# Attention scores mirrored once per sequence, and z turned later: one core of Trainium2

## The chip, the cores and the metric

The kernel runs on one core of a Trainium2 chip. The metric is the device time of one execution in microseconds (us). A core has five engines that run side by side and wait for each other through semaphores: TensorE (PE in the profile, with its weight loads as a lane of their own, PEld), VectorE (DVE), ScalarE (ACT), GpSimd (POOL) and SyncE (SP). SyncE and GpSimd also issue the DMA transfers, each from a queue of its own that works in order.

## The reference

There are 8 sequences of 2816 tokens. Attention without a softmax comes first, and its output is routed through a mixture of experts:

```python
scores = scale * np.matmul(z, z.transpose(0, 2, 1))   # z: 8 x 2816 x 64
attn = np.maximum(scores, 0.0) ** 2
x = u * np.matmul(attn, v)                            # u, v: 8 x 2816 x 256
...
y_dense = np.maximum(x @ w1_dense, 0.0) @ w2_dense
expert_idx = np.argmax(x @ w_gate, axis=1)            # 8 experts
y_moe = gate_w * (np.maximum(x @ w1[e], 0.0) @ w2[e]) # for the rows of expert e
out = y_dense + y_moe
```

What matters for this case: the scores are z times its own transpose, so the matrix of a sequence is symmetric. The block of scores of tokens i against tokens j is the transpose of the block of j against i.

## The kernel before

A sequence is 22 blocks of 128 tokens (`nK`). Six *groups* per sequence (`groups`) take 2, 4, 4, 4, 4 and 4 of these blocks as queries; a group's tile `A` holds relu-squared scores of all 22 key blocks against the group's queries. Three buffers hold `A` in turn, so group n + 3 overwrites group n.

`scores` makes one tile of scores: it takes a pair of PSUM banks, and TensorE multiplies blocks of `zT` (L390), keys as weights, the group's queries as the moving operand. 64 rows of the array carry the even key blocks and 64 the odd ones, side by side. `relu` then has ScalarE or VectorE take the relu into `r` (L405, L407), and ScalarE, VectorE or GpSimd the square into `A` (L418, L420). A tile of a four-block group is two matmuls of 512 columns; that of a two-block group is four of 256.

`av` makes the output of two query blocks: 88 matmuls of 256 columns with blocks of `A` as weights and `v` as the moving operand (L579), in two passes over the 22 key blocks. In between, `fill` puts in score tiles of this group or of the next two; `swap_rows` does so at the change of passes. At its end a VectorE multiplication by `u` (`gate_x`, L606, "the gate") writes `pays` and frees the output's banks, and SyncE turns the result into `xT` for the routing (L608). Ahead of each `av`, `load_u` has SyncE load `u` for two blocks further on into `ut` (L146), a tile with three buffers, so that a load waits for the gate of the `av` just ended.

Symmetry is used in part already: group n doesn't compute its scores against the keys of group n - 2 of its sequence (`far`). `far_steps` has SyncE transpose them by DMA (L468) out of `A` of group n - 2, into the place in `A` of group n where they belong. Before group n + 3 may be opened, these reads of group n's buffer have to be issued (`open_group`) and thought done (`read_at`).

The next sequence's z is loaded by GpSimd (`load_z`), copied by VectorE in two halves with each block doubled (`turn_z`, L113), and each half transposed by SyncE into `zT` (L116). Once the second half is issued, the sequence is entered in `z_there`, and from then on `ahead` may give out its scores.

All of this stands in an order that the kernel writes out itself at build time, for TensorE, ScalarE, VectorE and SyncE. A planner in the program keeps a clock of TensorE's work (`now`) and of the other engines (`free`), offers operations to them with guessed durations (`offer`, `best`, `run`), and so decides what is emitted next; each engine then runs its instructions in the emitted order. `tick(g)` runs what is due at block g: once in the middle of an `av` and once at its end. `soon(t, fn)` offers `fn` to VectorE at tick t. Here that holds the loads of z, v and the experts' weights (`wall`, 8 experts of 2048 columns) and the turns of z: the z load at block 0 of the sequence before, its turns at blocks 5 and 6, the loads of v from block 13, the weights from sequence 1 on at blocks 15, 18 and 21.

After the attention, the MoE stage (`slot`, `up`, `down`, `half`) runs over the tokens sorted by expert.

Of the kernel before, what the change touches and what calls it, by code (L numbers as in the profile page):

```python
# [15 lines left out]
P = 128  # L16
# [3 lines left out]
def kernel(  # L20
# [39 lines left out]
    WD = 2 * F + 4 * D  # L60
# [28 lines left out]
    wall = const.tile([P, E, WD], BF, name="wall")  # L89
# [13 lines left out]
    def load_z(b):  # L103
        z_of[b] = zpool.tile([P, nK, dq], BF, name="zr", bufs=1)
        nc.vector.memset(z_of[b][:, 0, 0:1], 0.0)
        nc.gpsimd.dma_start(out=z_of[b][:], in_=z[b].rearrange("(p k) d -> p k d", p=P))

    def turn_z(b, k0, k1):

        if k0 == 0:  # L110
            zn_of[b] = zpool.tile([P, nK, 2, dq], BF, name="zn", bufs=1)
            zT_of[b] = zpool.tile([P, nK, P], BF, name="zT")
        nc.vector.tensor_copy(  # L113
            zn_of[b][:, k0:k1, :, :],
            z_of[b][:, k0:k1, :].unsqueeze(2).to_broadcast([P, k1 - k0, 2, dq]))
        nc.sync.dma_start_transpose(  # L116
            out=zT_of[b][:, k0:k1, :],
            in_=zn_of[b][:, k0:k1].rearrange("p k h d -> p (k h d)"))
        if k1 == nK:
            z_there.add(b)  # L120

# [11 lines left out]
    now = [0.0]  # L133
# [4 lines left out]

    z_of, zn_of, zT_of, v_of, ut_of, xT_of, lg_of, rs = {}, {}, {}, {}, {}, {}, {}, {}

    def load_u(g, gate=False):
        ut = aw.tile([P, 2, D], F32, name="ut", bufs=3)
        if gate:
            nc.vector.memset(ut[:, 0, 0:1], 0.0)
        b, i = divmod(g, nK)
        nc.sync.dma_start(out=ut[:], in_=uf[:, b, i:i + 2, :])  # L146
        ut_of[g] = ut[:]


# [114 lines left out]
    A = {}  # L264
    groups = []
# [63 lines left out]
    def until(cond):  # L329

        while cond() is None:
            pick = best()
            assert pick is not None
            now[0] = max(now[0], pick[0][0])
            give(pick)
        now[0] = max(now[0], cond())
        run(now[0])
# [15 lines left out]
    def open_group(n):  # L353
        if n not in A:
            while turning and turning[0][0] <= n - 3:
                turning.pop(0)[1]()
            A[n] = aA.tile([P, nK, 4 * P], BF, name="A", tag="A")[:]
            w = groups[n][2]
            if w < 4:
                A[n] = A[n].rearrange("p k c -> p (k c)")[:, :nK * w * P]  # L360
                A[n] = A[n].rearrange("p (k c) -> p k c", k=nK)
# [78 lines left out]
        ts = [key_at.get((m, k)) for k in range(i0, i0 + w)]  # L440
        return None if None in ts else max(ts)

    def turned_to(a, n):

        _, j0, wj = groups[a]
        w = groups[n][2]
        flat = A[n].rearrange("p k c -> p (k c)")
        return flat[:, j0 * w * P:(j0 + wj) * w * P]

    def block(n, k, c):  # L450

        _, i0, w = groups[n]
        for a in far[n]:
            _, j0, wj = groups[a]
            if j0 <= k < j0 + wj:
                x = c * wj + k - j0
                return turned_to(a, n)[:, x * P:(x + 1) * P]
        return A[n][:, k, c * P:(c + 1) * P]

    def far_steps(a):  # L460

        _, j0, wj = groups[a]

        def step(n):
            _, i0, w = groups[n]
            assert a + 1 in A
            open_group(n)
            nc.sync.dma_start_transpose(  # L468
                out=turned_to(a, n).rearrange("p (x c) -> p x c", c=P),
                in_=A[a][:, i0:i0 + w, :].rearrange("p k c -> p (k c)"))  # L470
# [8 lines left out]
    turn_at = [0.0]  # L479
    read_at = {}  # L480
    jobs = []

    def fill(n, force=False):

        if jobs and jobs[0][0] <= now[0] and room(1):
            jobs.pop(0)[1]()
            return True
        m = ahead(n)
        busy = sum(1 for op in todo if op[0] in (1, 4))
        if m is not None and room(1) and busy <= (4 if n < 2 else 2):  # L490
            scores(m, left[m].pop(0))
            return True
        return False
# [59 lines left out]
    def av(n, i, between):  # L553
        b, i0, w = groups[n]
        if i == i0:
            turning.extend(far_steps(n))
        keep[0] = 0
        if n == 0 and i == i0:

            fill(n)  # L560
            need(n, 0)
        until(lambda: pairs[0][0] if pairs else None)
        ox = take_pair()
        o = banks(ox, "o")
        for p in range(2):
            rest = list(range(nK))
            for x in range(nK):
                k = rest[0]
                if i == i0 and p == 0:

                    k = min(rest, key=lambda k: (max(key_at.get((n, k), 9e9), v_at(n, k)), k))
                    need(n, k)
                rest.remove(k)
                if n == 0 and i == i0 and p == 0 and x in (12, 14, 16):
                    load_u(2 * (x - 12) // 2, gate=True)
                for h in range(2):
                    r = slice(h * dq, (h + 1) * dq)
                    j = p ^ h
                    nc.tensor.matmul(out=o[:, j, 0:D], lhsT=block(n, k, i + j - i0)[r],  # L579
                                     rhs=v_of[b][r, k, :], start=(p == 0 and x == 0),  # L580
                                     stop=(p == 1 and x == nK - 1))
# [12 lines left out]
        def done(t):  # L594
            give_pair(t + 0.1, ox)

        g = b * nK + i
        offer(now[0] + 0.2, 0, {"dve": (0.63, lambda eng: gate_x(g, o))}, done)
        keep[0] = 0


    def gate_x(g, o):
        g0 = g % (2 * G)
        x = pays[:, g0:g0 + 2, 0:D]
        assert g + 1 < 2 * G or (g - 2 * G in placed and g + 1 - 2 * G in placed)
        nc.vector.tensor_mul(x, o[:, :, 0:D], ut_of.pop(g))  # L606
        xT = aw.tile([P, 5, P], BF, name="xT", bufs=8)
        nc.sync.dma_start_transpose(  # L608
            out=xT[:], in_=pays[:, g0:g0 + 2, :].rearrange("p n r -> p (n r)")[:, 0:5 * P])
        for j in range(2):  # L610
            xT_of[g + j] = xT[:, 3 * j:3 * j + 2, :]

# [399 lines left out]
    def soon(t, fn, dur=0.07):  # L1012
        at(t, lambda: offer(now[0], 3, {"dve": (dur, lambda eng: fn())}))
# [19 lines left out]
    for e in range(E):  # L1033
# [62 lines left out]
    for q in range(nQ - 2):  # L1096
        t = starts[q + 1] - 1 + LAG
# [40 lines left out]
    for s in range(NT - MAYBE + 2):  # L1138
# [4 lines left out]
        if s % 3 == 1 and waiting:  # L1143
# [5 lines left out]
    n = nc.values_load(used[0:1, 0:1], min_val=0, max_val=NH,  # L1149
                       skip_runtime_bounds_check_because="made by the table")  # L1150
# [34 lines left out]
```

## Time and profile before

| | us |
|---|---|
| median of 3 runs | 883.23 (883.2 to 883.38) |
| the profiled execution | 883.35 |
| its span, first to last instruction | 881.2 |
| first to last matmul | 1.1 to 871.3 |
| end of the last attention output | about 555 |
| mean granted TensorE clock | 0.997 of full |

The profile's page gives busy time per engine, the chain of work that ended last, and groups of instructions by line with count, total and mean duration and the idle time ahead of them. Further views list stretches of time (busy time by engine, granted clock, the share of time in which the 16 DMA engines were busy), instructions in order of time, and waits. In a timeline "SPq" is SyncE's queue: the duration there is that of issuing a DMA, not of its transfer. Rows of instructions that follow each other are merged, "x32" being their number.

| SyncE's DMAs in the attention | line | count |
|---|---|---|
| `u` loads, 256 KB | L146 | 88 |
| `xT` transposes, 5 blocks of 128x128 | L608 | 88 |
| `A` to `A` transposes, 8 or 16 blocks | L468 | 32 |
| `zT` transposes, 11 blocks | L116 | 14 |

### The profile page before, as it was taken

The page shows a single profiled execution, that of the slowest core. Times are in us where ns is not written, and L with a number is a line of the kernel's source. Part 1 is how long each engine was busy: PE and PEld are TensorE (multiplying, and loading weights), DVE is VectorE, ACT ScalarE, POOL GpSimd, SP SyncE. Part 2 cuts the span into 40 slices and gives each one's busy share as a digit, 9 for nine tenths or more (in the row PEclk, how much of TensorE's full clock was granted, in tenths as well). Part 3 has the DMA queues.
Part 4 walks back from the last instruction along what each step waited for, and adds up shares of the span by engine and source line. Part 5 has one row for each costly group of instructions (what it writes and reads, how often), then busy time and mean ns, then how long its engine had stood idle before and what let it go on. Part 6 is the DMA issues. An engine that isn't in the chain of part 4 may idle for free.

```text
span 881.2 us, 30493 instructions
## 1 busy us (share of the span) xinstructions
PE 861.5 (98%) x12257; PEld 757.7 (86%) x12257; DVE 700.9 (80%) x1348; ACT 737.2 (84%) x913; POOL 491.6 (56%) x560
## 2 busy tenths in 40 slices
PE   7999999999999999999999999999999999999995
PEld 5788898898888888888888888888888888889994
DVE  7999999998999999999999996756665445446663
ACT  7999998998998998998998994577777777777773
POOL 8203355445426436436336334588888888877664
PEclk9999999999999999999999999999999999999998
DMA  8897988979979979989999976465646565533442
GB/s 155 148 151 139 161 162 149 185 165 173 181 161 185 167 165 185 162 181 143 198 182 165 165 135 115 104 136 131 136 122 120 121 123 122 124 103 103 95 98 76
DMA packets 258830, 127.62 MB, mean 145 GB/s; under 512 B 222846, under 2 KB 237438, under 8 KB 258688
## 3 DMA queue, kind: packets, MB, share of 16 engines
q1 hardware_dynamic: 227040, 70.23, 46.2%
q0 software_dynamic: 31648, 55.45, 29.6%
q8 instruction: 96, 1.57, 0.8%
q14 instruction: 46, 0.38, 0.1%
HBM read 61.54 MB, written 37.16 MB: 112 GB/s over the span
## 4 chain that ended last, share of the span: by engine, by line
PE 81%; POOL 6%; issue 4%; DVE 4%; DMA 2%; ACT 1%; SPq 0%; POOLq 0%; DVEq 0%; ACTq 0%
PE o L579 44%; PE h_ps L936 13%; PE yy L944 12%; PE s L390 10%; POOL out_dram L962 5%; DMA out_dram<-ring,ix 1%; DVE r L407 1%; PE lg L634 1%; POOL A L420 1%; DVE A L420 1%; ACT r L405 1%; DMA ring<-xs 1%; DVE pays L606 0%; ACT A L418 0%; DMA z<-in_z_dram 0%
## 5 line engine op out<-in xcount | busy, mean ns | idle before, releaser
L579 PE MATMUL o<-vb,A 64*128 64x256 bf16 x7744 | 491.1, 269 | 3.3 <-POOL A L420 1.7
L579 PEld LDWEIGHTS <-A 64*128 64x128 bf16 x7744 | 406.5, 94 | 53.7 <-POOL A L420 3.0
L724 POOL DMA_INDIRECT xs<-pays,pi x176 | 190.2, 1081 | 249.3 <-DVE pi L722 204.5
L405 ACT ACTIVATE r<-s 128x1024 f32<-128x1024 f32 (+1 forms) x268 | 263.8, 1012 | 21.6 <-PE s L390 19.2
L418 ACT ACTIVATE A<-r 128x1024 bf16<-128x1024 f32 (+1 forms) x263 | 266.6, 1046 | 7.1 <-DVE r L407 4.2
L939 ACT ACTIVATE ring<-h_ps 128x1024 bf16<-128x1024 f32 x180 | 184.1, 1024 | 89.6 <-PE h_ps L936 88.1
L407 DVE TENSOR_SCALAR r<-s 128x1024 f32<-128x1024 f32 (+1 forms) x164 | 197.6, 1215 | 6.5 <-PE s L390 1.9
L420 DVE TENSOR_TENSOR A<-r 128x1024 bf16<-128x1024 f32 x161 | 196.4, 1231 | 2.1 <-ACT r L405 1.7
L960 DVE SCALAR_TENSOR_TENSOR ring<-yy,me,ring 128x256 f32<-128x256 f32 x180 | 86.9, 483 | 124.6 <-ACT ring L959 84.7
L962 POOL DMA_INDIRECT out_dram<-ring,me x140 | 147.5, 1054 | 42.0 <-issue 24.4
L390 PE MATMUL s<-zT 64*128 64x512 bf16 (+1 forms) x944 | 156.8, 357 | 1.8 <-ACT zT L192 0.6
L944 PEld LDWEIGHTS <-ring 128*128 128x128 bf16 x1440 | 140.1, 98 | 16.1 <-issue 0.3
L944 PE MATMUL yy<-w2d,ring 128*128 128x256 bf16 x720 | 108.0, 273 | 0.1
L944 PE MATMUL yy<-ring 128*128 128x256 bf16 x720 | 108.0, 273 | 0.0
L936 PE MATMUL h_ps<-ring,w1d 128*128 128x256 bf16 x720 | 93.3, 272 | 1.0 <-DVE pays L606 0.8
L936 PE MATMUL h_ps<-ring 128*128 128x256 bf16 (+1 forms) x880 | 93.7, 253 | 0.0
L924 DVE COPY ring<-wall 128x2048 bf16 x110 | 79.7, 740 | 8.0 <-DVE ring L960 4.0
L936 PEld LDWEIGHTS <-ring 128*128 128x128 bf16 x880 | 74.3, 98 | 6.8
L936 PEld LDWEIGHTS <-w1d 128*128 128x128 bf16 x720 | 70.1, 98 | 9.3 <-issue 1.0
L390 PEld LDWEIGHTS <-zT 64*128 64x128 bf16 x944 | 57.6, 94 | 16.5 <-issue 2.6
L606 DVE TENSOR_TENSOR pays<-o,ut 128x512 bf16<-128x512 f32 x88 | 60.4, 687 | 14.0 <-PE o L579 13.7
L959 ACT COPY ring<-yy 128x256 f32<-128x256 f32 x180 | 65.9, 366 | 1.8 <-PE yy L944 1.8
(120 smaller groups left out, 370.0 us busy)
## 6 DMA issues: line engine op xcount, KB each, us to landing
ut<-in_u_dram SPq DMA_DIRECT2D x88, 256.0 KB
vb<-in_v_dram POOLq DMA_DIRECT2D x42, 192.0 KB
wall<-in_moe_w_dram POOLq DMA_DIRECT2D x16, 256.0 KB
xs<-pays,pi POOLq DMA_INDIRECT x176
zr<-in_z_dram POOLq DMA_DIRECT2D x7, 352.0 KB
out_dram<-ring,me POOLq DMA_INDIRECT x140
ring<-xs SPq DMA_TRANSPOSE x114
vb<-in_v_dram POOLq DMA_DIRECT2D x14, 128.0 KB
```

The lines of the kernel that those rows point to most:

```text
L390: nc.tensor.matmul(out=s[:, h, y * c:(y + 1) * c], lhsT=zT[r, k + h, :], rhs=zT[r, i0:i0 + w, :], start=True, stop=True)
L405: nc.scalar.activation(r[:, :, :c], s[:, :, :c], AF.Relu, scale=1.0 / S)
L407: nc.vector.tensor_scalar(out=r[:, :, :c], in0=s[:, :, :c], scalar1=1.0 / S, scalar2=0.0, op0=ALU.mult, op1=ALU.max)
L418: nc.scalar.activation(a, r, AF.Square)
L420: (nc.gpsimd if eng == "pool" else nc.vector).tensor_mul(a, r, r)
L579: nc.tensor.matmul(out=o[:, j, 0:D], lhsT=block(n, k, i + j - i0)[r], rhs=v_of[b][r, k, :], start=(p == 0 and x == 0), stop=(p == 1 and x ...
L724: ins = nc.gpsimd.indirect_dma_start(out=xs, out_offset=bass.IndirectOffsetOnAxis(ap=pi[:], axis=0), in_=pays[:, g % (2 * G), 0:ROW].bitca ...
L936: nc.tensor.matmul(out=h_ps[:, f, hs, :], lhsT=w1(c, f), rhs=xT[:, hs, c, :], start=(c == 0), stop=(c == 1))
L939: nc.scalar.activation(h, h_ps[:].rearrange("p f h t -> p f (h t)"), AF.Relu)
L944: nc.tensor.matmul(out=y[:, k, :], lhsT=h[:, f, j * P:(j + 1) * P], rhs=w2(f), start=(f == 0), stop=(f == 3))
L960: nc.vector.scalar_tensor_tensor(out=ys, in0=y[:, 1, :], scalar=me[:, j, 0:1], in1=yd, op0=ALU.mult, op1=ALU.add)
L962: ins = nc.gpsimd.indirect_dma_start(out=out, out_offset=bass.IndirectOffsetOnAxis(ap=ids[j], axis=0), in_=ys, in_offset=None, bounds_chec ...
```

## The change

Group 0 of each sequence but the last is now transposed into all later groups of its sequence from 2 on, not only into group 2. As the buffers of groups 3, 4 and 5 aren't there yet, these *mirrors* go into columns of `wall` that belong to the last two experts and are loaded later (`spare`, `mirror`); the mirrors for groups 4 and 5 are one transpose of 16 blocks, that for group 3 one of 8. `block` then gives the output matmuls their weights from there, and `left` holds three score tiles fewer per sequence. In sequence 7 no mirrors are made.

A new clock `sync` counts SyncE's guessed work: each DMA it issues adds a duration (`issue`). It takes the place of `turn_at` in deciding when the next transpose out of `A` may be issued; the time when a group's buffer is thought read (`read_at`) and when transposed scores are thought there (`key_at`) follow it too.

From sequence 1 on, z of the next sequence is loaded at block 7 in place of 0, and its halves are turned at blocks 10 and 13 in place of 5 and 6; sequence 0 keeps the old places. The weight loads of the last three halves of experts move into sequence 7, to blocks 4, 9 and 14, since the mirrors of sequence 6 must have been read by then.

```diff
@@ turn_z
         nc.sync.dma_start_transpose(
             out=zT_of[b][:, k0:k1, :],
             in_=zn_of[b][:, k0:k1].rearrange("p k h d -> p (k h d)"))
+        issue(1.5)
         if k1 == nK:
             z_there.add(b)
...
+    sync = [0.0]
+
+    def issue(dur, ready=0.0):
+        sync[0] = max(sync[0], now[0], ready) + dur
+
...
+    spare = wall[:].rearrange("p e w -> p (e w)")
+    mirror = {(0, 4): (E - 1) * WD, (0, 5): (E - 1) * WD + 8 * P, (0, 3): (E - 2) * WD + 2 * F}
+
+    def slots(b):
+
+        return list(mirror) if b < B - 1 else []
+
     left, far, key_at = {}, {}, {}
     for n, (b, i0, w) in enumerate(groups):
-        far[n] = [m for m in (n - 2,) if m >= 0
-                  if groups[m][0] == b]
+        far[n] = [m for m in range(max(n - 5, 0), n - 1)
+                  if groups[m][0] == b and (m == n - 2 or (m % 6, n % 6) in slots(b))]
...
-    def turned_to(a, n):
+    def turned_to(a, n, w):
 
         _, j0, wj = groups[a]
+        if a == n - 2:
+            flat = A[n].rearrange("p k c -> p (k c)")
+            return flat[:, j0 * w * P:(j0 + wj) * w * P]
+        x = mirror[a % 6, n % 6]
+        return spare[:, x:x + w * wj * P]
...
-        def step(n):
-            _, i0, w = groups[n]
-            assert a + 1 in A
-            open_group(n)
+        def step(ns):
+            n = ns[0]
+            i0, w = groups[n][1], sum(groups[m][2] for m in ns)
+            if n == a + 2:
+                open_group(a + 1)
+                open_group(n)
             nc.sync.dma_start_transpose(
-                out=turned_to(a, n).rearrange("p (x c) -> p x c", c=P),
+                out=turned_to(a, n, w).rearrange("p (x c) -> p x c", c=P),
                 in_=A[a][:, i0:i0 + w, :].rearrange("p k c -> p (k c)"))
-            turn_at[0] = now[0] + 0.17 * w * wj
-            read_at[a] = now[0] + 1.5 + 0.19 * w * wj
-            for j in range(wj):
-                key_at[n, j0 + j] = now[0] + 7.0
-
-        return [(a, lambda n=n: step(n), n) for n in (a + 2,) if a in far.get(n, [])]
+            issue(0.18 * w * wj, read_at.get(a - 1, 0.0) if n == a + 2 else 0.0)
+            read_at[a] = sync[0] + 3.5
+            for m in ns:
+                for j in range(wj):
+                    key_at[m, j0 + j] = sync[0] + 3.0
+
+        ns = [[n] for n in range(a + 2, min(a + 6, len(groups))) if a in far[n]]
+        if len(ns) == 4:
+            ns[2:] = [ns[2] + ns[3]]
+        elif groups[a][2] == 4:
+            ns = ns[1:] + ns[:1]
+        return [(a, lambda m=m: step(m), m[-1]) for m in ns]
...
-                if x in (3, 10, 17)[1 - p:] and turning and turn_at[0] <= now[0]:
+                if x in (3, 10, 17)[1 - p:] and turning and sync[0] <= now[0] + 0.5:
                     t = can_turn(turning[0][2], turning[0][0])
-                    if t is not None and t <= now[0] and turning[0][0] + 1 in A:
+                    if t is not None and t <= now[0]:
                         turning.pop(0)[1]()
...
-            soon(t, lambda b=b: load_z(b + 1))
-            soon(t + 5, lambda b=b: turn_z(b + 1, 0, nK // 2), 0.4)
-            soon(t + 6, lambda b=b: turn_z(b + 1, nK // 2, nK), 0.4)
+            soon(t + 7 if b else 0, lambda b=b: load_z(b + 1))
+            soon(t + 10 if b else 5, lambda b=b: turn_z(b + 1, 0, nK // 2), 0.4)
+            soon(t + 13 if b else 6, lambda b=b: turn_z(b + 1, nK // 2, nK), 0.4)
...
-    ts = [b * nK + x for b in range(1, B) for x in (15, 18, 21)][2:]
+    ts = [b * nK + x for b in range(1, B - 1) for x in (15, 18, 21)][2:-1]
+    ts += [(B - 1) * nK + x for x in (4, 9, 14)]
```

The `u` load and the `xT` transpose call `issue` too (0.6 and 1.25 us).

More of the change, by code (lines that the diff above doesn't have):

```diff
@@ L146, in load_u @@
         nc.sync.dma_start(out=ut[:], in_=uf[:, b, i:i + 2, :])
+        issue(0.6)
         ut_of[g] = ut[:]
@@ L441, in can_turn, with block @@
         return None if None in ts else max(ts)
-    def turned_to(a, n):
+    def turned_to(a, n, w):
         _, j0, wj = groups[a]
+        if a == n - 2:
[3 more added lines that the diff above has]
+        return spare[:, x:x + w * wj * P]
+    def block(n, k, c):
         w = groups[n][2]
-        flat = A[n].rearrange("p k c -> p (k c)")
-        return flat[:, j0 * w * P:(j0 + wj) * w * P]
-    def block(n, k, c):
-        _, i0, w = groups[n]
         for a in far[n]:
@@ L456, in block @@
                 x = c * wj + k - j0
-                return turned_to(a, n)[:, x * P:(x + 1) * P]
+                return turned_to(a, n, w)[:, x * P:(x + 1) * P]
         return A[n][:, k, c * P:(c + 1) * P]
@@ L462, in far_steps @@
         _, j0, wj = groups[a]
-        def step(n):
-            _, i0, w = groups[n]
-            assert a + 1 in A
-            open_group(n)
+        def step(ns):
[4 more added lines that the diff above has]
+                open_group(n)
             nc.sync.dma_start_transpose(
-                out=turned_to(a, n).rearrange("p (x c) -> p x c", c=P),
+                out=turned_to(a, n, w).rearrange("p (x c) -> p x c", c=P),
                 in_=A[a][:, i0:i0 + w, :].rearrange("p k c -> p (k c)"))
-            turn_at[0] = now[0] + 0.17 * w * wj
-            read_at[a] = now[0] + 1.5 + 0.19 * w * wj
-            for j in range(wj):
-                key_at[n, j0 + j] = now[0] + 7.0
-        return [(a, lambda n=n: step(n), n) for n in (a + 2,) if a in far.get(n, [])]
+            issue(0.18 * w * wj, read_at.get(a - 1, 0.0) if n == a + 2 else 0.0)
[9 more added lines that the diff above has]
+        return [(a, lambda m=m: step(m), m[-1]) for m in ns]
     turning = []
-    turn_at = [0.0]
     read_at = {}
@@ L609, in gate_x @@
             out=xT[:], in_=pays[:, g0:g0 + 2, :].rearrange("p n r -> p (n r)")[:, 0:5 * P])
+        issue(1.25)
         for j in range(2):
@@ L1023 @@
         if b + 1 < B:
-            soon(t, lambda b=b: load_z(b + 1))
-            soon(t + 5, lambda b=b: turn_z(b + 1, 0, nK // 2), 0.4)
-            soon(t + 6, lambda b=b: turn_z(b + 1, nK // 2, nK), 0.4)
+            soon(t + 7 if b else 0, lambda b=b: load_z(b + 1))
+            soon(t + 10 if b else 5, lambda b=b: turn_z(b + 1, 0, nK // 2), 0.4)
+            soon(t + 13 if b else 6, lambda b=b: turn_z(b + 1, nK // 2, nK), 0.4)
             for h in range(8):
                 soon(t + 13 + 5 * h // 7, lambda b=b, h=h: load_v(b + 1, h, 8))
-    ts = [b * nK + x for b in range(1, B) for x in (15, 18, 21)][2:]
+    ts = [b * nK + x for b in range(1, B - 1) for x in (15, 18, 21)][2:-1]
+    ts += [(B - 1) * nK + x for x in (4, 9, 14)]
+    assert len(ts) == 2 + 2 * E
     soon(ts.pop(0), lambda: dense(w1d, moe_w1_dense, 2))
```

## The prediction

> **What bounds the kernel now.** I read the totals by engine first, then the busy time by stretches, then the chain that ended last.
>
> ```profile
> span 881.2 us, 30493 instructions
> PE 861.5 (98%) x12257; PEld 757.7 (86%) x12257; DVE 700.9 (80%) x1348; ACT 737.2 (84%) x913; POOL 491.6 (56%) x560
> PE 81%; POOL 6%; issue 4%; DVE 4%; DMA 2%; ACT 1%; SPq 0%; POOLq 0%; DVEq 0%; ACTq 0%
> ```
>
> ```profile
> core 0: us, PE busy (x) PEld busy (x) DVE busy (x) ACT busy (x) POOL busy (x), PEclk, DMA share, GB/s
> 0.00:60.00 60.00, 53.64 (x803) 43.42 (x805) 53.89 (x72) 53.71 (x57) 24.80 (x35) 1.00 0.87 152
> ...
> 240.00:300.00 60.00, 59.91 (x1016) 52.85 (x1015) 57.02 (x107) 55.98 (x61) 28.23 (x32) 1.00 0.96 172
> 420.00:480.00 60.00, 59.91 (x1027) 52.06 (x1024) 56.79 (x109) 55.87 (x62) 25.74 (x29) 1.00 1.01 180
> ```
>
> The change lies in the attention, which lasts until about 555 us. From 60 us on TensorE is busy 59.9 of every 60 us at the full clock, so there a microsecond of its work removed is a microsecond gained, and a microsecond in which it waits is one lost: nothing later has idle time to give back. VectorE and ScalarE stand at 56 to 57 of 60, so they are mostly behind their plan, not ahead of it. The DMA engines show shares near 1, so landings there are not quick.
>
> **The mirrors: work removed.** By the order of instructions, 42 matmuls of scores go (768 of 512 columns become 726), that is 21 tiles, three for each of sequences 0 to 6; with each goes one relu and one square. The 7744 output matmuls stay; 336 of them read their weights from `wall` instead of `A`.
>
> ```profile
> 60.84 0.22 PE s L390 x2
> ...
> 61.97 1.75 PE o L579 x32
> ```
>
> In the chain in order of time one tile of scores (two matmuls of 512 columns, side by side on two halves of the rows) takes 0.22 us, and an output matmul of 256 columns 1.75 / 32 = 0.0547 us. 21 x 0.22 = **4.6 us gained**. The 42 relus and squares, 1.0 to 1.2 us each, shorten engines that are not the bound; I count nothing for them. Only in the first 60 us, where TensorE idles 6.4 us, could they free some of sequence 0's share; at most that, and I take 0.
>
> Two mirrors of each sequence are added to SyncE's queue, 8 and 16 blocks of 128x128.
>
> ```profile
> L468 SPq DMA_TRANSPOSE A<-A x32: 1254/2154/5825, 11.9 to 521.5; - x32
> ```
>
> At the least and median rows that is 1.25 + 2.15 = 3.4 us of issuing more per sequence of 67 us, on a queue that mostly stands waiting; their readers come 25 us or more later. The last one must land before group 3's first square overwrites group 0's buffer; that stands in the rivals. Moving three weight loads to blocks 4, 9 and 14 of the last sequence shifts GpSimd's issues and nothing TensorE waits for before the MoE stage; 0, covered by the 8 blocks still to come.
>
> **The z turn: a new wait.** This step decides. Before, both halves of the next sequence's `zT` are turned at blocks 5 and 6:
>
> ```profile
> 313.32 0.88 DVE L113 COPY zn<-zr 128x1408 bf16<-128x1408 bf16 x1
> ...
> 314.22 3.35 SPq L116 DMA_TRANSPOSE zT<-zn  x2
> ...
> 315.30 0.88 DVE L113 COPY zn<-zr 128x1408 bf16<-128x1408 bf16 x1
> ```
>
> ```profile
> L390 PE MATMUL s<-zT x20: 266/269/279, 330.9 to 335.8; 64*128 64x256 bf16 x20
> ```
>
> Issued by 317.57, first needed by the scores of the next sequence's narrow group (the 256-column form) at 330.9: 13 us of cover. After, the second copy is offered at the end of block 12 (tick 13), `z_there` is set in the same call, and the planner, which gives the landing no time, puts the next sequence's scores at once into block 14. Counting the new order for the turns in sequences 1 to 6 (sequence 0 keeps blocks 5 and 6), X being the end of block 12's output matmuls:
>
> - for sequences 2, 3, 5 and 6 TensorE reaches the weight load of z block 11, the first of the second half, after 16 output matmuls and 11 score matmuls of 256 columns: 27 x 0.0547 = 1.48 us after X;
> - for sequences 4 and 7 after 44 and 11: 55 x 0.0547 = 3.0 us.
>
> That load waits on the second transpose, and all matmuls of block 14 stand behind it. What must happen first is a chain. In the first four cases VectorE's order is copy, then block 12's gate (L606), and SyncE's is the `u` load (L146), which waits for that gate because it reuses its `ut` buffer, and only then the transpose.
>
> ```profile
> 304.57 0.69 DVE L606 TENSOR_TENSOR pays<-o,ut 128x512 bf16<-128x512 f32 x1 [0.16 <-PE o L579]
> ...
> 305.29 0.33 SPq L146 DMA_DIRECT2D ut<-in_u_dram  x1
> ...
> 305.71 1.21 SPq L608 DMA_TRANSPOSE xT<-pays  x1
> ```
>
> So from a gate's start to the next transpose on SyncE are 305.71 - 304.57 = 1.14 us. How long a transpose takes from issue to landing, no row of `zT` shows, so it is bounded by others:
>
> ```profile
> 1.28 2.64 DMA z<-in_z_dram
> ...
> 562.31 4.99 DMA ring<-xs
> ```
>
> ```profile
> SPq L468 <- DMA A<-A: 2.0, 1, 2.0
> ```
>
> ```profile
> 423.70 1.31 SPq L468 DMA_TRANSPOSE A<-A  x1
> ...
> 431.29 4.46 SPq L468 DMA_TRANSPOSE A<-A  x1
> ```
>
> A plain load landed in 2.64 us on empty queues; an 8-block transpose under load only 7.59 us after its start (the one issued at 431.29 waited its last 2.0 us for it); a 4-block transpose in the chain took 4.99. I take 4.99, as the nearest kind, and 2.64 and 7.59 as ends.
>
> Cases one: copy 0.88 from X, 1.14 to the transpose, 4.99 to the landing = X + 7.0; less 1.48 leaves TensorE standing **5.5 us**. Least: copy already done at X, landing 2.64: 1.14 + 2.64 - 1.48 = 2.3. Most: VectorE one relu late (1.22, the L407 row's mean), landing 7.59: 9.35.
> Cases two: copy after the gate, but SyncE has the `xT` transpose (1.21) ahead, so it issues at X + 2.4; landing X + 7.4; less 3.0 leaves **4.4 us**, ends 2.0 and 8.2.
>
> ```profile
> L407 DVE TENSOR_SCALAR r<-s 128x1024 f32<-128x1024 f32 (+1 forms) x164 | 197.6, 1215 | 6.5 <-PE s L390 1.9
> ```
>
> Sum of the stalls: 4 x 5.5 + 2 x 4.4 = **30.8 us**, ends 13.2 and 53.8. The first half, copied three ticks earlier, is needed 0.22 us after X at the earliest, about 8 us after its copy against 0.88 + 1.39 (below) + a landing: at worst it waits less than the second, and the two waits overlap, so 0. The z load itself goes from block 0 to block 7 of a sequence, a block and a half (about 9 us) before the first copy, more than the 7.59 of the slowest landing: 0; were it late, VectorE would stand on it with all gates and relus queued behind.
>
> ```profile
> L116 SPq DMA_TRANSPOSE zT<-zn x14: 1262/1388/2582, 41.0 to 451.1; - x14
> ```
>
> Span: 881.2 - 4.6 + 30.8 = 907.4. The profiled execution took 883.35 us with its span of 881.2, and the median of the three runs is 883.23, so 2.1 us lie around the span: **909.5 us**.
>
> **The clock after a stall.** A stall this long could also cost clock.
>
> ```profile
> 871.00:873.00 2.00, 0.27 (x3) 0.00 (x0) 0.81 (x2) 0.37 (x1) 1.70 (x2) 1.00 0.54 145
> 873.00:875.00 2.00, 0.00 (x0) 0.00 (x0) 0.00 (x0) 0.00 (x0) 0.61 (x2) 1.00 0.24 58
> 875.00:877.00 2.00, 0.00 (x0) 0.00 (x0) 0.00 (x0) 0.00 (x0) 0.47 (x1) 0.51 0.02 0
> ```
>
> ```profile
> 1.14 2.53 PE L162 MATMUL warm<-ones 128*128 128x128 bf16 x22 [1.14 <-DVE ones L158]
> ```
>
> The last matmul ends at 871.27, and the granted clock falls to 0.5 at 875.0, 3.8 us later. At the start, 22 matmuls of 128 columns over all rows take 2.53 us; at the attention's pace (256 columns on both halves of the rows in 0.109 us) they would take 22 x 0.0547 = 1.2, so the start runs at half pace. The Trainium skill, "TensorE: Matmul & The Clock Gate", Part 1, says that the clock halves after an idle window of about 3.4 us, windows running free of the program, and comes back after as long a busy one. The tail of this trace agrees; no idle stretch inside the attention is there to test it.
>
> **The rivals.**
>
> 1. *The clock falls in each stall* (the skill's rule, carried through). If after each of six stalls the 3.8 us of the tail run at half pace, each loses 1.9 us: 909.5 + 11.4 = 920.9. For it: my stalls are longer than 3.8 us. Against: 4.4 and 5.5 are only just longer. 0.22.
> 2. *The mirrors jam SyncE.* Group 3's first square on VectorE is about 8.8 us of TensorE work behind the 16-block mirror in the order; such a transpose can issue for 4.46 us (above) and land 6.3 after that. With 2 us until it starts, it lands 12.8 us on, 4 us late, seven times; VectorE then holds score banks and TensorE follows: up to 28 us more, 937. It decides once the landing passes 8.8 us. Against: the median issue is 2.15. 0.08.
> 3. *Faster: the stalls are covered.* If the second half of `zT` lands within 1.48 and 3.0 us of X, because VectorE copies well before X and the `u` load finds its gate done, only the mirrors' gain stays: 883.35 - 4.6 = 878.8. It turns faster below a stall of 4.6 / 6 = 0.77 us each. Against: 2.64 us for the quickest landing alone, and VectorE busy 57 of 60. 0.07; in between, within 0.2%, 0.03.
>
> That the mirrors are not used is excluded by the order.
>
> **How the numbers follow.** The forecast's own case has 0.60. The range 892 to 928 takes its lower end from the least stalls (881.2 - 4.6 + 13.2 + 2.1 = 892) and reaches past rival 1; all six stalls at their most (932.5) I leave out. About 0.2 lie outside. Within 0.2% (1.8 us) this kernel's runs can't be told apart; faster 0.07, same 0.03, slower 0.90.
>
> **What would show it.** Score matmuls 902 in place of 944, at 0.22 us a tile; in each of six sequences one TensorE idle stretch of 4 to 6 us at the scores' weight load from `zT`, about 1.5 or 3 us into block 14, ended by the DMA into `zT`; full busy slices otherwise; gates followed by `u` load, then that transpose. Rival 1 shows granted clock under 1 behind these stretches, rival 2 waits of VectorE on `wall`'s transposes. I am wrong if TensorE's idle time at those loads is under 1 us each, or if idle time appears elsewhere in the attention.

## The result, and the profile after

The changed kernel takes **922.12 us** (median of 4 runs, 920.67 to 924.25) against 883.31 us for the kernel before, measured beside it (4 runs, 883.2 to 884.28): a ratio of 1.0439, 95% interval 1.0417 to 1.0461. It is slower. The forecast was 909.5 us with a range of 892 to 928; rival 1, the same stalls with the clock falling behind each of them, stood at 920.9.

The page of the changed kernel, its first lines and the shares of the chain that ended last:

```profile
span 920.0 us, 30370 instructions
...
PE 869.7 (95%) x12216; PEld 760.9 (83%) x12216; DVE 682.1 (74%) x1332; ACT 716.4 (78%) x887; POOL 496.4 (54%) x560
...
PE 62%; DVE 9%; DMA 7%; issue 7%; POOL 6%; ACT 6%; POOLq 0%; SPq 0%; DVEq 0%; ACTq 0%
```

The span grew by 38.8 us and TensorE's share fell from 98% to 95%. In the windows of 60 us (the third figure from the end of a row is the granted clock) the stretches that had 59.91 us of TensorE before now have four to five us less, at a lower clock; the first 60 us are as they were (53.64 before):

```profile
0.00:60.00 60.00, 53.68 (x805) 43.45 (x807) 53.98 (x72) 53.75 (x57) 24.80 (x35) 1.00 0.96 165
...
240.00:300.00 60.00, 54.84 (x916) 47.27 (x913) 47.98 (x98) 46.42 (x52) 26.11 (x28) 0.97 0.95 161
...
420.00:480.00 60.00, 55.95 (x920) 47.49 (x916) 48.39 (x101) 46.85 (x52) 25.94 (x31) 0.94 1.01 169
```

Two groups of the page say where it waits (busy us, mean ns of one, then the idle time just before and what ended most of it). The squares of VectorE at L434 wait for a mirror 2.4 us in all; the scores at L404, 902 matmuls now, wait 30.2 us for the DMA into `zT`:

```profile
L434 DVE TENSOR_TENSOR A<-r 128x1024 bf16<-128x1024 f32 (+1 forms) x152 | 182.8, 1214 | 5.7 <-DMA wall<-A 2.4
L404 PE MATMUL s<-zT 64*128 64x512 bf16 (+1 forms) x902 | 153.8, 361 | 33.4 <-DMA zT<-zn 30.2
```

One of the six boundaries (into sequence 4), in the timeline (start, duration, engine, what, in brackets the idle time before):

```profile
272.84 0.68 DVE L629 TENSOR_TENSOR pays<-o,ut 128x512 bf16<-128x512 f32 x1
...
273.50 0.88 DVE L113 COPY zn<-zr 128x1408 bf16<-128x1408 bf16 x1
273.55 0.33 SPq L152 DMA_DIRECT2D ut<-in_u_dram  x1
...
274.23 1.72 SPq L631 DMA_TRANSPOSE xT<-pays  x1
...
276.06 1.38 SPq L116 DMA_TRANSPOSE zT<-zn  x1
...
280.06 0.28 PE L404 MATMUL s<-zT 64*128 64x256 bf16 x1 [4.63 <-DMA zT<-zn]
```

The gate (L629), the copy of the second half (L113), on SyncE the `u` load and the `xT` transpose, then the turn of `zT` at 276.06; TensorE has run out of work that may go ahead of that load and stands 4.63 us until the turn lands. The same kernel's windows over that place (each row gives the window, its length, the busy time of TensorE's matmuls and weight loads, VectorE, ScalarE and GpSimd, and ends with granted clock, DMA share and GB/s):

```profile
275.00:277.00 2.00, 0.43 (x7) 0.11 (x3) 1.29 (x2) 1.17 (x2) 1.76 (x1) 1.00 0.70 181
277.00:280.00 3.00, 0.00 (x0) 0.00 (x0) 0.00 (x0) 0.00 (x0) 2.46 (x4) 1.00 0.92 160
280.00:281.00 1.00, 0.94 (x16) 0.79 (x18) 0.18 (x1) 0.62 (x1) 0.00 (x0) 0.85 1.12 153
281.00:284.00 3.00, 3.00 (x32) 2.18 (x30) 2.19 (x3) 1.35 (x2) 0.55 (x1) 0.50 0.51 76
284.00:286.00 2.00, 2.00 (x36) 1.59 (x33) 1.01 (x6) 1.55 (x3) 0.00 (x0) 0.97 0.53 93
```

The clock is still 1.00 while TensorE stands, and 0.50 from 281 to 284, when it is busy without a break. It does 32 matmuls in those 3 us, where 3 us hold 55 at 0.0547 each.

All six boundaries show the stall and the fall of the clock. By the trace TensorE's idle stretches there are 3.9, 1.5 + 2.6, 4.6, 5.8, 3.9 and 7.8 us, and to each boundary belongs a stretch of half clock, four of 3.4 us, one of 6.8 and one of 10.2. At two boundaries it begins 0.6 and 0.9 us after the stall, at the other four inside it. Of these 30.7 us TensorE was busy 22.3, so at half pace it lost 11.2. The sum of the span: 38.8 = 30.2 of waits for `zT` + 11.2 of clock - 4.6 of mirrors + 2.0 that are left over. TensorE's busy time on the two pages puts the clock somewhat higher: it rose by 8.2 us although 4.6 us of its work went, 12.8 in all, so most of what is left over is busy time too.

### The profile page after: what moved, and what is told of

Its sections match the earlier page's. It is cut to its first block, busy times and chain, and to the rows that moved or that the text cites. A ratio compares the mean times of both kernels' runs of the same rounds, so it can differ in the third digit from the quotient of the medians.

```text
span 920.0 us, 30370 instructions
## 1 busy us (share of the span) xinstructions
PE 869.7 (95%) x12216; PEld 760.9 (83%) x12216; DVE 682.1 (74%) x1332; ACT 716.4 (78%) x887; POOL 496.4 (54%) x560
## 4 chain that ended last, share of the span: by engine, by line
PE 62%; DVE 9%; DMA 7%; issue 7%; POOL 6%; ACT 6%; POOLq 0%; SPq 0%; DVEq 0%; ACTq 0%
PE o L602 30%; PE h_ps L960 12%; PE yy L968 12%; PE s L404 6%; POOL out_dram L986 5%; DVE r L421 4%; DMA zT<-zn 3%; ACT A L432 3%; ACT r L419 3%; DVE A L434 3%; DMA wall<-A 2%; DMA out_dram<-ring,ix 1%; DVE pays L629 1%; POOL A L434 1%; PE lg L658 1%
## 5 line engine op out<-in xcount | busy, mean ns | idle before, releaser
L602 PE MATMUL o<-vb,A 64*128 64x256 bf16 x7408 | 480.5, 273 | 3.3 <-ACT A L432 2.0
L602 PEld LDWEIGHTS <-A 64*128 64x128 bf16 x7408 | 395.4, 95 | 51.2 <-POOL A L434 3.1
L748 POOL DMA_INDIRECT xs<-pays,pi x176 | 195.0, 1108 | 252.7 <-DVE pi L746 205.0
L419 ACT ACTIVATE r<-s 128x1024 f32<-128x1024 f32 (+1 forms) x254 | 249.9, 1013 | 81.7 <-PE s L404 78.3
L432 ACT ACTIVATE A<-r 128x1024 bf16<-128x1024 f32 (+1 forms) x251 | 255.7, 1053 | 3.3 <-DVE r L421 2.5
L421 DVE TENSOR_SCALAR r<-s 128x1024 f32<-128x1024 f32 (+1 forms) x157 | 189.2, 1212 | 45.9 <-PE s L404 42.3
L434 DVE TENSOR_TENSOR A<-r 128x1024 bf16<-128x1024 f32 (+1 forms) x152 | 182.8, 1214 | 5.7 <-DMA wall<-A 2.4
L404 PE MATMUL s<-zT 64*128 64x512 bf16 (+1 forms) x902 | 153.8, 361 | 33.4 <-DMA zT<-zn 30.2
L404 PEld LDWEIGHTS <-zT 64*128 64x128 bf16 x902 | 57.4, 95 | 51.2 <-DMA zT<-zn 32.1
L629 DVE TENSOR_TENSOR pays<-o,ut 128x512 bf16<-128x512 f32 x88 | 61.1, 694 | 28.5 <-PE o L602 28.2
L130 POOL DMA_DIRECT2D vb<-in_v_dram x60 | 33.5, 561 | 67.8 <-DVE vb L129 45.8
```

Source lines behind the costliest of these rows:

```text
L404: nc.tensor.matmul(out=s[:, h, y * c:(y + 1) * c], lhsT=zT[r, k + h, :], rhs=zT[r, i0:i0 + w, :], start=True, stop=True)
L419: nc.scalar.activation(r[:, :, :c], s[:, :, :c], AF.Relu, scale=1.0 / S)
L421: nc.vector.tensor_scalar(out=r[:, :, :c], in0=s[:, :, :c], scalar1=1.0 / S, scalar2=0.0, op0=ALU.mult, op1=ALU.max)
L432: nc.scalar.activation(a, r, AF.Square)
L434: (nc.gpsimd if eng == "pool" else nc.vector).tensor_mul(a, r, r)
L748: ins = nc.gpsimd.indirect_dma_start(out=xs, out_offset=bass.IndirectOffsetOnAxis(ap=pi[:], axis=0), in_=pays[:, g % (2 * G), 0:ROW].bitca ...
```

## The experiments

There are twelve more runs, on three chips. On those of e1 to e4 and of e5 to e8 the kernel before itself takes 921 us, on that of e9 to e12 883 to 885 us, as in the first measurement. So each ratio is to runs of the kernel before on the same chip, and times are compared only within a chip. The expectations of e1 to e4 name times for a chip at 883 us; they are read here as ratios to it.

**e1: z as before, everything else as changed.**

```diff
-            soon(t + 7 if b else 0, lambda b=b: load_z(b + 1))
-            soon(t + 10 if b else 5, lambda b=b: turn_z(b + 1, 0, nK // 2), 0.4)
-            soon(t + 13 if b else 6, lambda b=b: turn_z(b + 1, nK // 2, nK), 0.4)
+            soon(t, lambda b=b: load_z(b + 1))
+            soon(t + 5, lambda b=b: turn_z(b + 1, 0, nK // 2), 0.4)
+            soon(t + 6, lambda b=b: turn_z(b + 1, nK // 2, nK), 0.4)
```

> The changed kernel with one part undone: z loaded at block 0 and turned at blocks 5 and 6 in every sequence, as before; mirrors and SyncE's clock stay. If the late turn is the cause of all of the loss (theory A), the 30 us of TensorE waits on the DMA into zT go, the granted clock stays at 1.00 through the attention, and what is left is the mirrors' gain of 4.6 us: 878 to 880 us, ratio to before 0.994 to 0.997. If the mirrors crowd SyncE or the DMA engines (rival B), the time stays over 890 with waits of VectorE on the transposes into wall. If the new clock of SyncE orders the far scores badly (rival C), TensorE waits appear elsewhere and the time lies above 884.

Measured: 947.92 us against 921.05, ratio 1.0306 (1.0259 to 1.0353). A miss: undoing the z edit does not give the mirrors' gain, it gives another loss. The waits (us in all, times, longest) between 60 and 530 us hold none for `zT`, but these:

```profile
DVE A L434 <- DMA wall<-A: 16.6, 5, 5.0
PE s L404 <- DVE r L421: 14.6, 7, 4.9
...
ACT A L432 <- DMA wall<-A: 4.5, 3, 3.2
```

The square that writes into group 0's old buffer waits until the last mirror has read it, the relus queue behind it on VectorE, and TensorE waits for the relus. That is rival 2 of the prediction, which the changed kernel hardly shows. Why it appears here was open until e10.

**e2: the kernel before with z loaded at block 7 and turned at 10 and 13,** nothing else (the three lines of the change put into the kernel before).

> The kernel before with one part of the change alone: z loaded at block 7 and turned at blocks 10 and 13 from sequence 1 on; no mirrors, old clock. Theory A: the turn costs by itself what it costs in the change, six TensorE stalls of 3 to 7 us at the scores' weight load from zT and a fall of the clock behind most of them, less where the order puts some work between the second turn and its first reader (2.2 us there in four sequences, 1.3 and 1.6 in two, against 1.2 to 1.5 in the change): 915 to 925 us. Rival B (the mirrors are at fault): 883 to 887.

Measured: 964.31 us, ratio 1.0449 (1.0404 to 1.0494).

```profile
PEld L390 <- DMA zT<-zn: 32.4, 6, 10.5
PE s L390 <- DMA zT<-zn: 30.8, 6, 10.3
```

The z edit alone, without mirrors and without the clock of SyncE's work, brings the six waits, of 2.6 to 10.3 us, and the whole loss (expected: 1.036 to 1.047).

**e3: the turns where the change puts them, but the planner told of the new z two ticks later.**

```diff
-        if k1 == nK:
+        if k1 == nK and b == 1:
             z_there.add(b)
...
+            if b:
+                at(t + 15, lambda b=b: z_there.add(b + 1))
```

> The changed kernel with one line moved: the turns stay at blocks 10 and 13, but the next sequence's scores are given out only from the end of block 14 (tick 15). The second half's first reader then stands 7.7 to 8.5 us of TensorE work behind the turn, against 1.2 to 1.5. Theory A: a landing takes 6 to 7 us from there, so the stalls shrink to 0 to 1 us each, the clock holds: 878 to 886 us. If the cost lay in the DMA traffic of a late turn and not in who waits for it, or if the scores that start a half block later then come short, the time stays over 890.

**e4: the second turn one tick earlier** (block 12 in place of 13).

> The changed kernel with the second turn one tick earlier (12 in place of 13). Its first reader stands 1.3 and 2.5 us behind it in two sequences and 3.5 us in four (1.2 to 1.5 in the change). Theory A: the stalls shrink by these differences to some 4, 3 and four times 2 to 3.5 us (about 18 us in all), and most become too short for the clock to fall: 895 to 903 us. If the clock falls at each stall whatever its length, 905 to 908. If the stall doesn't depend on this distance: 918 to 924.

Measured: e3 926.15 us, ratio 1.0041 (1.0008 to 1.0074); e4 929.85 us, ratio 1.0081 (1.0045 to 1.0117). The waits of e3, then of e4:

```profile
PEld L404 <- DMA zT<-zn: 7.4, 4, 3.4
...
PE s L404 <- DMA zT<-zn: 6.3, 4, 3.2
```

```profile
PEld L404 <- DMA zT<-zn: 12.4, 6, 3.6
PE s L404 <- DMA zT<-zn: 10.7, 6, 3.3
```

By the author's count in the order of instructions, TensorE has 1.2 to 1.5 us of work between the second turn and its first reader in the changed kernel, 1.3 to 3.5 in e4, and 7.7 to 8.5 in e3. The wait falls with that cover, 30.2, 10.7, 6.3 us, and the stretches of half clock in the attention with it, from six to two and one. As a ratio e4 was expected at 1.013 to 1.022 and lost less, its waits being 10.7 us and not about 18. e3 was expected at 0.994 to 1.003 and just misses that: one turn landed 9.2 us after its issue there, and TensorE stood 3.2 us in spite of the cover. e3 also shows that the loss hangs on who waits for the late turn and not on the turn itself, which stands where the change puts it.

**e5: the changed kernel** beside e6, e7 and e8.

> The changed kernel, unchanged, beside the three others on one chip. Theory A (the late second z transpose stalls TensorE at each of six boundaries and the granted clock halves behind each stall): six idle stretches of 2.5 to 8 us at the scores' weight load, 28 to 34 us together, six stretches of half clock, and a ratio to the kernel before of 1.040 to 1.048 on whichever chip it is. Theory B (a good part of the 38.8 us comes from how that one chip answers, not from the change): ratio outside 1.035 to 1.050, with idle stretches that differ from those of the first trace by more than a third.

Measured: 963.92 us against 920.87, ratio 1.0477 (1.0421 to 1.0532). By the trace its idle stretches over 0.4 us between 60 and 545 us sum to 31.8 us (31.7 in the first trace), and it has six stretches of half clock, 44.4 us, of which it is busy 29.7, so 14.9 lost, against 11.2 in the first trace. The sum of the stalls is the same on a chip where the kernel before takes 921 us.

**e6: z loaded at block 4, turned at blocks 7 and 9.**

```diff
-            soon(t + 7 if b else 0, lambda b=b: load_z(b + 1))
-            soon(t + 10 if b else 5, lambda b=b: turn_z(b + 1, 0, nK // 2), 0.4)
-            soon(t + 13 if b else 6, lambda b=b: turn_z(b + 1, nK // 2, nK), 0.4)
+            soon(t + 4 if b else 0, lambda b=b: load_z(b + 1))
+            soon(t + 7 if b else 5, lambda b=b: turn_z(b + 1, 0, nK // 2), 0.4)
+            soon(t + 9 if b else 6, lambda b=b: turn_z(b + 1, nK // 2, nK), 0.4)
```

> The changed kernel with the z load at block 4 instead of 7 and the two z transposes at blocks 7 and 9 instead of 10 and 13; 10.5 us of TensorE's work then lie between the second transpose and its first reader (1.2 to 1.5 us in the changed kernel), and the z load is issued well behind the mirrors. Theory A (what e1 paid was its z load at block 0, which fell on the mirrors' transposes; mirrors by themselves cost nothing): no idle stretch over 2 us at a boundary, at most one stretch of half clock, waits of VectorE and ScalarE on the mirrors under 6 us in all, ratio 0.992 to 1.003. Theory B (the mirrors themselves crowd SyncE, whatever z does): waits of VectorE and ScalarE on the mirrors of 12 us or more and a ratio of 1.015 to 1.035, as in e1.

Measured: 913.54 us, ratio 0.9914 (0.9881 to 0.9948): 0.5 to 1.2% faster than the kernel before. The groups of its page:

```profile
L434 DVE TENSOR_TENSOR A<-r 128x1024 bf16<-128x1024 f32 (+1 forms) x165 | 196.3, 1203 | 4.4 <-DMA wall<-A 1.9
...
L404 PE MATMUL s<-zT 64*128 64x512 bf16 (+1 forms) x902 | 150.3, 356 | 2.8 <-PE s L404 0.9
```

With all mirrors in place the scores wait for no transpose, and VectorE waits 1.9 us for mirrors. So mirrors as such do not crowd SyncE.

**e7: the clock of SyncE's work alone:** no mirrors, z at blocks 0, 5 and 6 (the three z lines as in e1).

```diff
-        return list(mirror) if b < B - 1 else []
+        return []
...
```

> The changed kernel without any mirror (each group has only its far group, as before) and with z loaded at block 0 and turned at blocks 5 and 6, as before; the clock of SyncE's work and the times at which weights are loaded stay as changed. Theory A (SyncE's clock by itself moves far scores by little): TensorE's work as before, ratio 0.997 to 1.004. Theory B (e1's 27 us came from the order that the clock gives, not from the mirrors): ratio 1.015 to 1.035 with idle stretches at scores that wait for VectorE.

Measured: 921.79 us, ratio 1.0000 (0.9966 to 1.0033). The order that the new clock gives changes the time by no more than 0.34%, some 3 us either way. e1 differs from e7 by the mirrors alone, and its ratio is 0.031 higher.

**e8: the kernel before,** for its trace on the chip of e5 to e7.

> The kernel before, for its trace on the same chip as the three others. If the chip is as the first one: 883 us, span 881, TensorE idle under 2 us in all between 60 and 860 us. If it is the one of the first four experiments: 918 to 927 us, with 15 to 22 us of idle stretches of about 1 us each at the second expert product between 560 and 860 us, which wait for the sums that GpSimd scatters; none of these belongs to the change.

Measured: 919.88 us, span 917.8. Its windows, and then those of the kernel before in the first measurement:

```profile
60.00:540.00 480.00, 476.35 (x8077) 415.33 (x8073) 453.21 (x836) 447.56 (x491) 210.33 (x227) 1.00 0.92 164
540.00:860.00 320.00, 296.87 (x2898) 259.21 (x2893) 165.53 (x379) 203.64 (x317) 232.59 (x270) 1.00 0.48 109
```

```profile
60.00:540.00 480.00, 478.06 (x8148) 418.05 (x8145) 457.24 (x848) 451.36 (x494) 211.05 (x229) 1.00 0.93 165
540.00:860.00 320.00, 318.71 (x3198) 286.45 (x3194) 182.60 (x414) 224.62 (x350) 246.24 (x288) 1.00 0.53 118
```

The attention (first row) runs nearly alike; the MoE stage (second row) has 21.8 us less of TensorE in the same time. This chip is slower there, in work that the change doesn't touch.

**e9: the stalls filled with matmuls,** to part idle time from clock.

```diff
+    filled = set()
...
                 r = slice(h * dq, (h + 1) * dq)
+                if b > 1 and b not in filled and k + h >= nK // 2:
+                    filled.add(b)
+                    for _ in range(42):
+                        nc.tensor.matmul(out=s[:, h, y * c:(y + 1) * c], lhsT=ones[r, :],
+                                         rhs=zT[r, i0:i0 + w, :], start=True, stop=True)
```

> The changed kernel with 42 more matmuls of 256 columns at each of the six boundaries, put on TensorE just ahead of the first score that reads the second half of the new zT; they read ones and the first half of zT and write a part of the score tile that the score then overwrites, so nothing of the result changes. By the rate of the scores they take about 4.5 us, as long as the stall that they fill. Theory A (of the changed kernel's loss some 11 us is the granted clock that halves behind each idle stretch): idle left at the boundaries 4 to 9 us in all, at most two stretches of half clock, and in spite of some 3 us by which the filling is longer than a stall the time falls 5 to 10 us against the changed kernel of the same call. Theory B (what is lost beside the idle time has nothing to do with the clock): no fall, time within 2 us of the changed kernel or 2 to 5 us above it.

**e11: the changed kernel beside it.**

> The changed kernel once more, as the measure for e9 on the same chip: ratio 1.040 to 1.053 by theory A and by theory B; it tells nothing by itself.

Measured: e9 916.29 us, ratio 1.0356 (1.0342 to 1.0370); e11 922.72 us, ratio 1.0435 (1.0414 to 1.0457). The intervals are apart: 6.4 us less. The waits of TensorE in e11, then in e9, and last the group of the filling in e9:

```profile
PE s L404 <- DMA zT<-zn: 28.2, 8, 7.2
```

```profile
PE s L411 <- DMA zT<-zn: 7.1, 3, 4.1
```

```profile
L409 PE MATMUL s<-zT,ones 64*128 64x256 bf16 x252 | 32.9, 294 | 0.0
```

Waiting and filling together are 40.0 us in e9, 11.8 more than e11's wait of 28.2, and yet the kernel is faster: what it got back is the clock. Its trace has two stretches of half clock, 17.1 us, where e11 has six with 30.7. The profiled execution of e9 is its slowest, 921.61 us; over its six executions the mean granted clock is 0.988 to 0.994, over the five of e11 0.975 to 0.979. Theory A holds, though the filling was 5.5 us a boundary and not 4.5, mostly because one of the two stretches fell on it: there a filling matmul started every 0.213 us, at the other boundaries every 0.109, which is also the measure of half pace.

**e10: e6 with the z load back at block 0.**

```diff
-            soon(t + 4 if b else 0, lambda b=b: load_z(b + 1))
+            soon(t, lambda b=b: load_z(b + 1))
```

> As e6, but with the z load back at block 0 (e6 has it at block 4); the z transposes stay at blocks 7 and 9. Theory A (e1's pauses came from the z load, issued 0.1 us from the second mirror transpose and moving bytes while that one runs): waits of VectorE and ScalarE on the mirrors of 10 us or more, second mirror transposes that land 9 us or more after their issue, ratio 1.010 to 1.035. Theory B (they came from e1's early z transposes at blocks 5 and 6, which SyncE must fit between mirrors and far scores): as e6, ratio 0.988 to 1.000 and waits on the mirrors under 6 us.

Measured: 913.25 us against 883.44, ratio 1.0335 (1.0319 to 1.0351). The z load's place alone makes the difference between e6's gain and a loss of 30 us. (The profiled execution was the fastest, 902.37 us.) Its waits, and the worst place in its timeline:

```profile
DVE A L434 <- DMA wall<-A: 18.5, 5, 9.0
PE s L404 <- DVE r L421: 16.1, 5, 8.2
...
ACT A L432 <- DMA wall<-A: 11.7, 3, 8.0
```

```profile
367.69 13.62 SPq L486 DMA_TRANSPOSE wall<-A  x2
```

```profile
368.38 0.57 POOL L106 DMA_DIRECT2D zr<-in_z_dram  x1 [0.20 <-issue]
```

```profile
386.22 2.86 SPq L486 DMA_TRANSPOSE A<-A  x1
386.25 1.06 ACT L432 ACTIVATE A<-r 128x1024 bf16<-128x1024 f32 x1 [8.02 <-DMA wall<-A]
386.62 1.22 DVE L434 TENSOR_TENSOR A<-r 128x1024 bf16<-128x1024 f32 x1 [8.96 <-DMA wall<-A]
...
389.09 0.61 PE L404 MATMUL s<-zT 64*128 64x512 bf16 x2 [8.20 <-DVE r L421]
```

SyncE starts the two mirrors at 367.69, GpSimd issues the z load 0.7 us later, the two mirrors take 13.6 us to issue, the squares wait 8 to 9 us and TensorE 8.2. In the six sequences the second mirror landed 9.2, 10.1, 10.0, 9.3, 15.5 and 7.2 us after its issue, and TensorE stood 1.1, 2.8, 2.7, 1.4, 8.2 and 0 us. The prediction's turning point for this wait, a landing past 8.8 us, fits all six. In e6 the same transposes landed in some 6 to 7.5 us.

**e12: e6 once more,** on another chip.

> e6 once more, in more rounds, to see whether it beats the kernel before on another chip too. Theory A (stalls and clock are gone, what stays is the gain of 42 matmuls of 512 columns, 4.6 us in the prediction): ratio 0.990 to 0.997, on a chip like the first one 875 to 881 us, no stretch of half clock between 60 and 540 us and idle of TensorE under 3 us there. Theory B (the gain seen with e6 was a chance of that chip): ratio 0.998 to 1.004 or above.

Measured: 879.15 us against 884.81, **ratio 0.9940** (0.9926 to 0.9953).

```profile
span 877.3 us, 30394 instructions
```

```profile
60.00:540.00 480.00, 477.36 (x8180) 421.18 (x8177) 439.23 (x846) 430.60 (x467) 210.23 (x233) 1.00 1.00 177
```

TensorE works 477.4 of these 480 us at the full clock, 478.1 before; the span is 3.9 us shorter than the 881.2 of the kernel before in the first measurement.

## Why the prediction was right, and where it was not

**The sign and the mechanism** are shown. The late second turn makes TensorE stand at six boundaries (the wait is named in the trace, e2 brings it alone, and e3, e4 and e6 make it smaller and then remove it as the cover grows).

**The sum of the stalls** was 30.8 us by the working and 30.2 by the waits. Its terms were less good than their sum. The four boundaries put at 5.5 us took 3.9, 4.1, 5.8 and 3.9; the two put at 4.4 took 4.6 and 7.8. The landing of the turn, taken as 4.99 us from another transpose in the chain, was 3.9 to 4.1 us in four and 5.8 and 7.6 in two. The issue of the turn was off as well. Counting X back from the stall by the working's 1.48 and 3.0 us (an estimate), it came some 0.5 us sooner than worked out at the four put at 5.5 us, where VectorE began the copy before X, and 1.2 and 0.8 us later at the two put at 4.4. All stalls lie within the ends that the working gave, but that their sum came out to 0.6 us is luck: the errors cancelled. The first half of z, put at 0, cost 1.5 us at one boundary.

**The clock** is the term that was mis-sized. The forecast's own case had it at nothing and kept it as rival 1 at 11.4 us, with a chance of 0.22, because stalls of 4 to 6 us seemed only just long enough. It fell at all six boundaries, also at those of 3.9 us, and cost 11.2 us; rival 1's 920.9 is 1.2 us from the result. That it is so near is partly luck: rival 1 took 3.8 us of half pace behind every stall, while the trace has stretches of 3.4 to 10.2 us in which TensorE was busy for 2.9 to 4.9, and in e5 and e11 they cost the same kernel 14.9 and 12.8 us. The argument against it was wrong: beside the 3.8 us of the kernel's tail, 4.4 and 5.5 were long enough already, and shorter stalls can be too, of 3.1 and 3.3 us in e4 and of 2.7 us in e10. Not every one is: in e2 a stall of just under 3 us left the clock at full.

**The mirrors** gain about what was worked out, 4.6 us: e12, which also holds the new clock of SyncE's work and the milder move of z, is 5.3 us faster by its ratio (4.2 to 6.5 by the interval), and e6 by 4.8 to 11.0. The relief of VectorE and ScalarE is worth nothing that shows, as taken: in e12 VectorE has 18 us less to do between 60 and 540 us, and TensorE is as full as before. The clock of SyncE's work is worth nothing by itself, within 3 us (e7).

**Rival 2,** mirrors that jam SyncE, did not decide in the changed kernel (2.4 us), but its price, "up to 28 us more", is near the 27 and 30 us that e1 and e10 lost once the z load falls on the mirrors, and its turning point fits e10. The way there was another: uneven stalls of 0 to 8.2 us in e10, with half clock behind three of them, and not 4 us seven times. The prediction took the move of the z load at 0, from the side of its readers, and did not see that leaving it at block 0 would have cost 30 us beside the mirrors. So the three z lines hold one edit that the mirrors need and one that costs some 43 us (38.8 + 4.6); moving only so far that both conditions are met (e6) gives the gain.

Open: why two chips are slower in the MoE stage, and which resource the z load and the mirrors share; neither was tried.

## What to carry to other kernels

When a planner marks data as there at the moment its transfer is issued, look for what it schedules next: at a boundary where the reader is 1.5 us away and the landing takes 4 to 8 (in e2 once 10.7), the reader stalls with all that is queued behind it. In three traces of the changed kernel the half clock cost 11.2, 12.8 and 14.9 us beside waits of 30.2, 28.2 and 29.4: a third to a half of the stalls' own time, to be added to it. And when a transfer is moved, ask which others it then runs beside, since a load that nobody waits for can make someone else's transpose land 2 to 8 us late.

## What the runs showed of the hardware that was not expected

The granted clock goes in steps of 3.41 us: every stretch of half clock in the attention is a whole number of them. And a step before a fall need not be idle. Around the boundary into sequence 3 of the changed kernel (busy TensorE, then clock):

```profile
198.78:202.19 3.41, 1.76 (x29) 1.00 1.06 129
202.19:205.60 3.41, 0.91 (x18) 1.00 0.89 183
205.60:209.02 3.42, 3.42 (x39) 0.50 0.24 30
209.02:212.43 3.41, 3.41 (x73) 1.00 0.70 108
```

A step that was 52% busy was followed by full clock, one that was 27% busy by half clock, though TensorE had gone back to work 0.9 us before. In e9 a step that was 42% busy did the same, and then fully busy steps did not bring the clock back at once (here the first busy time of a row is TensorE's, and the clock is the third figure from the end):

```profile
125.60:129.02 3.42, 1.45 (x28) 1.08 (x24) 2.01 (x5) 1.17 (x2) 1.16 (x2) 1.00 1.17 137
129.02:132.43 3.41, 3.41 (x23) 2.38 (x19) 0.75 (x1) 2.80 (x3) 0.00 (x0) 0.50 0.88 204
132.43:135.85 3.42, 3.42 (x18) 2.37 (x16) 0.00 (x0) 0.00 (x0) 0.00 (x0) 0.50 0.00 0
135.85:139.26 3.41, 3.41 (x25) 2.37 (x23) 0.37 (x1) 0.00 (x0) 0.00 (x0) 0.50 0.02 5
139.26:142.67 3.41, 3.41 (x33) 2.43 (x31) 1.22 (x4) 0.00 (x0) 1.57 (x2) 0.50 0.18 13
142.67:146.10 3.43, 3.43 (x75) 3.18 (x71) 2.97 (x9) 2.65 (x4) 1.88 (x3) 1.00 0.46 67
```

From 129.5 to 138.2 TensorE did the filling, matmuls on one half of the rows one after another; three steps of it passed at half clock, and only one step after the kernel's own matmuls, on both halves, did the clock return. At four other boundaries, where the clock had not fallen before it, the same filling held it at full. The Trainium skill, "TensorE: Matmul & The Clock Gate", Part 1, tells of windows of about 3.4 us, an idle one before the fall and a busy one before the return. The steps of 3.41 us agree with it, but here partly busy steps were enough to fall, and in e9 steps full of half-height matmuls were not enough to return.

Laid over all the traces of this case, from 60 us to the last matmul, the steps say more. Every full-clock step with TensorE busy for 36% or less was followed by half clock, none with 50% or more was, and between 42 and 49% both happened. In half clock, steps busy for 80% or more brought the full clock back, those of e9's filling apart, and steps of 77% or less did not. So how a short stall lies in the steps matters: the one in e2 that left the clock at full was spread over two steps, 58 and 56% busy. By an estimate from the same numbers, a stall of 3.9 us spread evenly over two steps leaves each 43% busy, so the stalls of the changed kernel were about as long as it takes for the clock to fall wherever they lie.
